# Chunked attention before two gated layers: its small products on all four 64x64 tiles of TensorE, on pairs of PSUM banks

## The chip, the cores and the metric

One core of a Trainium2 chip runs one program. The metric is the device time in microseconds (us); the profiled execution is a further run of the same program, of which the trace keeps every instruction. PE is TensorE's matrix multiply, PEld its weight load, DVE VectorE, ACT ScalarE, POOL GpSimd and SP SyncE, which issues the DMAs.

## The reference

The attention is a linear recurrence per head (4 batches, 8 heads, 768 steps, 48 numbers per head), and its output goes through two gated layers:

```python
for t in range(S):
    state = alpha[:, :, t, :, None] * state + np.einsum('bhd,bhe->bhde', k[:, :, t], v[:, :, t])
    y[:, :, t] = np.einsum('bhd,bhde->bhe', q[:, :, t], state)
x = y.transpose(0, 2, 1, 3).reshape(B * S, H * D)      # 3072 x 384
h = x @ w_in;  x = (h * np.cos(h)) @ w_out             # 384 -> 2048 -> 384
out = ((x @ w_a) * (x @ w_b)) @ w_o                    # 384 -> 1536 -> 384
```

The first line of the loop decays the state and adds the outer product of k and v of step t.

## The kernel before

**Units.** The recurrence is done in chunks of 64 steps. A unit is one chunk of one batch with all eight heads, as four pairs of heads (`NP`): 48 units, 12 chunks to a batch (`NCH`). One head of a pair lies on SBUF partitions 64 to 111, the other on 0 to 47 (`HEADS`). VectorE makes the running products of alpha with two scans (L289, L301), GpSimd scales q (L313), and k is scaled on VectorE in the first eight units and on GpSimd after (L326).

**Small products of a unit on TensorE** (K is the rows contracted, M the columns of weights loaded):
- T, the transposes of k (L359): 8 products, absent in a batch's last chunk, which leaves no state
- S, the scores of k with q (L369 and L372, a line per head of the pair): 8 products
- N, the new keys with v (L431, L432): 8 products, absent in a batch's last chunk
- Y, the outputs (L447, and L451 with the old state where it is carried on its own): 8 or 16 products
- O, the old state added by a product with the identity (L435): 1 product

These are float32, and each product stands in the trace as two matmuls. In T, S and N a product takes one 64x64 quarter of the array: the head on the upper partitions writes the lower half of PSUM's partitions or the other way round, so that of the four quarters two are used, on a diagonal. Y uses all rows of the array and half its columns.

**Banks.** T and N of a unit lie in one PSUM bank (`tu`), S and Y in another (`sy`); odd units of the first eight use two accumulator banks in their place (`tags`, L342). ACT reads T (copy of k, L364) and Y (L548, high part of x); DVE reads S (masking, L398 or L405), N (decay of the state L500, or an add L515) and Y (low part of x, L551).

**Kinds of units.** Units 0 to 15 (`APART`) carry the state apart (`s_t`); from unit 16 on the state stands in the rows of v that a unit's products read anyhow, so that there is no O and no L451. Units 0 to 7 are done first, since layer one needs 512 steps at once. From unit 8 on a unit is a *block* on TensorE, emitted in one go between the large products: Y of unit u, then T and S of unit u+1, then N and O of unit u (L473).

**Large products.** 3072 columns in six groups of 512 (`NG`). Layer one has 16 steps a group, each with nine 128x128x512 products into `hp` (L645) and nine into the accumulators (L652), with ACT and DVE making h cos(h) in between (L695 to L714). The first two steps of the first group are cut into halves of 256 columns, of which the first needs units 0 to 3 and the second units 4 to 7 (`mm_part`, L674). Weights arrive as 64-bit words and are converted by ACT, DVE and POOL (L588 to L625) while the first group runs. Layer two has 12 steps of 27 products.

**What sets the order.** Every operation is recorded with an estimated duration, its dependencies and a due time (`Plan`, L65), and a list scheduler writes out one fixed order per engine. At run time each engine works through its order and waits where something isn't ready. An operation whose estimate or dependencies are changed can so move others.

Of the kernel before, what the change touches and what calls it, by code (L numbers as in the profile page):

```python
# [51 lines left out]
IN_COLS = W_A + 2 * NE4  # L52
# [114 lines left out]
def chunked(ctx: ExitStack, tc: tile.TileContext, u_in: bass.AP, wts: bass.AP, out: bass.AP, in_range: bass.AP):  # L167
# [23 lines left out]
    mask = att.tile([P, 1, C], F32, name="mask", bufs=1)  # L191
    nc.gpsimd.memset(mask, 1.0)
    for r0 in (0, 64):
        nc.gpsimd.affine_select(
            out=mask[r0:r0 + 64], in_=mask[r0:r0 + 64], pattern=[[0, 1], [1, C]],
            compare_op=ALU.is_ge, fill=0.0, base=0, channel_multiplier=-1,
        )
# [63 lines left out]
    def plan_load(u):  # L261
# [3 lines left out]
        def load():  # L265
# [5 lines left out]
            cuts = (0, NA + 1, IN_COLS) if u == 0 else (0, IN_COLS)  # L271
# [70 lines left out]
    def tags(u):  # L342
        return ("acc1", "acc2") if u < UG and u % 2 else ("tu", "sy")

    def plan_scores(u, block=None):
        d, ops = un[u], U[u]
        apart = u < APART
        due = unit_due(u)
        m, kt = m_t[u % 3], k_t[u % 2]
        k, ma, m_before = ops["k"], ops["ma"], ops["m_before"]  # L350
        kp, kn_of = kt, kn_t[u % 2]
        state = u % NCH != NCH - 1
        tp = kn = None

        def transpose():
            d["tp"] = d["tu"][:, 0:NE4].rearrange("p (c e) -> p c e", e=D)
            for p in range(NP):
                for (rows, _), r0 in zip(HEADS, (0, 64)):
                    nc.tensor.matmul(  # L359
                        d["tp"][r0:r0 + 64, p, :], kp[rows, p, :], ident[rows, rows], start=True, stop=True  # L360
                    )

        def copy_k():
            nc.scalar.copy(kn_of[:, :, 0:D], d["tp"])  # L364

        def score():
            sc = d["sc"] = d["sy"][:, 0:256].rearrange("p (c t) -> p c t", t=C)
            for p in range(NP):
                nc.tensor.matmul(  # L369
                    sc[0:64, p, :], kp[64:112, p, :], m[64:112, 1 if apart else 0, p, :], start=True, stop=True  # L370
                )
                nc.tensor.matmul(  # L372
                    sc[64:128, p, :], kp[0:48, p, :], m[0:48, 2 if apart else 1, p, :], start=True, stop=True
                )

        def both():
            tu, sy = tags(u)
            d["tu"], d["sy"] = bank(tu, tu), bank(sy, sy)
            if state:
                transpose()  # L380
            score()

        if block is None:
            sc = op(PE, 0.95, both, [*k, *ma], due=due - 1.0)
            ops["tu"], ops["sy"] = (take(tag, 1, sc) for tag in tags(u))
        else:
            sc = block[0]
            need(sc, *k, *ma)
            ops["tu"], ops["sy"] = block[1:]
        ops["emit"] = ([transpose] if state else []) + [score]  # L390
        ops["k_last"] = [sc]
        if state:
            ops["kn"] = kn = op(ACT, 0.34, copy_k, [sc, *(U[u - 2]["us_op"] if u >= 2 else [])])
            ops["tu"] += [kn]
        if apart:
            mk = [op(
                DVE, 0.42,
                lambda: nc.vector.tensor_tensor(m[:, 0], d["sc"], mask.to_broadcast([P, NP, C]), op=ALU.mult),  # L398
                [sc, *m_before],
            )]  # L400
        else:
            mk = [
                op(
                    DVE, 0.42,
                    lambda r0=r0, i=i: nc.vector.tensor_tensor(  # L405
                        m[r0:r0 + 64, i], d["sc"][r0:r0 + 64], mask[r0:r0 + 64].to_broadcast([64, NP, C]), op=ALU.mult
# [706 lines left out]
```

## Time and profile before

| | us |
|---|---|
| median of 3 runs | 987.89 (987.19 to 987.96) |
| the profiled execution, own time | 988.87 |
| its span, first to last instruction | 987.2 |
| PE busy in it | 972.0 |
| DVE, ACT, POOL busy in it | 529.3, 407.6, 230.9 |

The span is 1.67 us less than the profiled execution's own time, and that execution is 0.98 us over the median. A busy share over the whole span says little here: the engines beside PE are busy in the first part and nearly idle in the last, so the profile is read by stretches.

### The profile page before, as it was taken

The numbers are of one execution on the slowest core, as the hardware profiler recorded it, in microseconds if no ns is written. First come the engines' busy times: TensorE is split into PE (matmuls) and PEld (weight loads), VectorE is DVE, ScalarE is ACT, GpSimd is POOL, SyncE is SP. The second block draws the span as 40 slices with busy tenths as digits, with TensorE's granted clock in tenths as the row PEclk, the third lists the DMA queues.
The fourth block names the chain that finished last, engine by engine and source line by source line (L and its number), as shares of the span: only waits on it lengthen the run. The fifth ranks groups of instructions, "written<-read, shape, count | busy, mean of one in ns | idle before, by whom it ended". The sixth has DMA issues, their size and how long they took to land.

```text
span 987.2 us, 16801 instructions
## 1 busy us (share of the span) xinstructions
PE 972.0 (98%) x6909; PEld 800.6 (81%) x6909; DVE 529.3 (54%) x887; ACT 407.6 (41%) x754; POOL 230.9 (23%) x259
## 2 busy tenths in 40 slices
PE   8899999999999999999999999999999999999996
PEld 6788888888888888888887888888888888888885
DVE  6998986766766676665877862222222222222221
ACT  4578854445445444544766532112112112112111
POOL 4556653313322322221323431001001001000000
PEclk8889999999999999999999999999999999999999
DMA  9355412112221211112223410000000000000000
GB/s 365 131 170 188 162 41 79 62 48 73 72 67 49 81 50 58 50 34 104 97 96 101 156 33 14 19 1 18 15 1 23 10 1 28 5 1 32 1 1 35
DMA packets 17700, 63.38 MB, mean 64 GB/s; under 512 B 2384, under 2 KB 4816, under 8 KB 17616
## 3 DMA queue, kind: packets, MB, share of 16 engines
q1 hardware_dynamic: 17616, 62.24, 18.3%
q8 instruction: 56, 0.92, 0.4%
q14 instruction: 28, 0.23, 0.1%
HBM read 55.15 MB, written 4.72 MB: 61 GB/s over the span
## 4 chain that ended last, share of the span: by engine, by line
PE 95%; DMA 2%; DVE 1%; SPq 0%; issue 0%; ACT 0%
PE acc L652 35%; PE hp L645 20%; PE bp L645 15%; PE ap L645 15%; PE sy L447 3%; PE tu L359 2%; PE sy L369 2%; DMA st_t<-wts 2%; PE tu L432 1%; DMA w_t<-u_in 1%; PE tu L431 1%; PE sy L451 0%; PE tu L435 0%; DVE wf_t L605 0%; DVE wf_t L599 0%; PE sy L372 0%
## 5 line engine op out<-in xcount | busy, mean ns | idle before, releaser
L652 PE MATMUL acc<-ghi_t,w_t 128*128 128x512 f32 x972 | 301.2, 391 | 0.0
L645 PE MATMUL hp<-x_t,w_t 128*128 128x512 f32 (+1 forms) x882 | 217.9, 392 | 3.1 <-DMA x_t<-x_t 3.1
L652 PEld LDWEIGHTS acc<-ghi_t,w_t 128*128 128x128 f32 x972 | 181.7, 188 | 37.7
L645 PEld LDWEIGHTS hp<-x_t,w_t 128*128 128x128 f32 x882 | 163.3, 191 | 37.0 <-issue 3.5
L808 DVE TENSOR_TENSOR bp<-c_t,bp 128x512 f32<-128x512 f32 x72 | 50.1, 695 | 262.0 <-PE bp L645 244.0
L652 PE MATMUL acc<-glo_t,w_t 128*128 128x512 f32 x486 | 189.3, 390 | 0.0
L645 PE MATMUL bp<-x_t,w_t 128*128 128x512 f32 x594 | 145.6, 389 | 0.0
L645 PE MATMUL ap<-x_t,w_t 128*128 128x512 f32 x540 | 132.2, 389 | 0.0
L645 PEld LDWEIGHTS bp<-x_t,w_t 128*128 128x128 f32 x594 | 111.5, 188 | 23.5
L645 PEld LDWEIGHTS ap<-x_t,w_t 128*128 128x128 f32 x540 | 101.4, 188 | 21.2
L805 ACT COPY c_t<-ap 128x512 f32<-128x512 f32 x72 | 42.3, 587 | 179.8 <-PE ap L645 179.6
L652 PEld LDWEIGHTS acc<-glo_t,w_t 128*128 128x128 f32 x486 | 91.2, 188 | 19.5
L812 ACT CAST ghi_t<-bp 128x512 fp32r<-128x512 f32 x72 | 42.3, 587 | 137.9 <-DVE bp L808 137.9
L768 POOL TENSOR_TENSOR x_t<-x,x_t 128x512 fp32r<-128x512 f32 x18 | 25.1, 1416 | 256.9 <-ACT x_t L765 256.9
L625 POOL TENSOR_TENSOR w_t<-wf_t,w_t 128x768 fp32r<-128x768 f32 x32 | 64.1, 2005 | 88.4 <-ACT w_t L614 78.7
L710 ACT CAST ghi_t<-hp 128x512 fp32r<-128x512 f32 x96 | 56.4, 587 | 68.2 <-DVE hp L706 67.3
L695 ACT ACTIVATE c_t<-hp 128x512 int32<-128x512 f32 x96 | 57.6, 600 | 58.1 <-PE hp L645 57.2
L698 DVE CUSTOM_DVE_ANT_0 c_t<-c_t,hp 128x512 f32<-128x512 int32 x96 | 65.6, 683 | 25.3 <-ACT c_t L695 24.9
L703 ACT ACTIVATE c_t<-c_t 128x512 f32<-128x512 f32 x96 | 60.4, 629 | 44.7 <-DVE c_t L698 44.2
L706 DVE TENSOR_TENSOR hp<-c_t,hp 128x512 f32<-128x512 f32 x96 | 65.9, 686 | 23.7 <-ACT c_t L703 23.2
L326 POOL TENSOR_TENSOR k<-ar_t,in_t 112x256 f32<-112x256 f32 x40 | 30.8, 769 | 201.8 <-PE sy L372 157.8
L714 DVE TENSOR_TENSOR glo_t<-hp,ghi_t 128x512 fp32r<-128x512 f32 x96 | 65.4, 681 | 18.4 <-ACT ghi_t L710 18.2
(110 smaller groups left out, 1094.2 us busy)
## 6 DMA issues: line engine op xcount, KB each, us to landing
st_t<-wts SPq DMA_DIRECT2D x34, 768.0 KB, 4.4
in_t<-u_in SPq DMA_DIRECT2D x40, 578.0 KB, 3.7
out<-o_t SPq DMA_DIRECT2D x18, 256.0 KB, 2.1
w_t<-u_in SPq DMA_DIRECT2D x7, 578.0 KB, 8.2
x_t<-x_t SPq DMA_DIRECT2D x48, 48.0 KB, 2.5
w_t<-u_in SPq DMA_DIRECT2D x1, 447.5 KB, 4.2
w_t<-u_in SPq DMA_DIRECT2D x1, 130.5 KB, 2.2
```

The costliest lines, as they stand in the source:

```text
L625: nc.gpsimd.tensor_tensor(t[:, 1], conv.pop(i), t[:, 0].bitcast(F32), op=ALU.subtract)
L645: nc.tensor.matmul(acc, wt[:, w, j * P:(j + 1) * P], r[:, j, :], start=i == 0, stop=i == len(terms) - 1)
L652: nc.tensor.matmul(accs[j], wt[:, w, j * P:(j + 1) * P], r, start=first and i == 0, stop=last and i == 2)
L695: nc.scalar.activation(s["c"].bitcast(I32), s["u"], AF.Identity, bias=-0.25, scale=-1.0)
L698: nc.vector._custom_dve(TENSOR_ADD_SAT, out=s["c"], in0=s["c"].bitcast(I32), in1=s["u"], s0=0.25, s1=-0.75)
L703: nc.scalar.activation(s["c"], s["c"], AF.Sin, bias=math.pi / 2, scale=TWO_PI)
L706: nc.vector.tensor_tensor(s["u"], s["c"], s["u"], op=ALU.mult)
L710: nc.scalar.copy(s["hi"], s["u"])
L714: nc.vector.tensor_tensor(s["lo"], s["u"], s["hi"].bitcast(F32), op=ALU.subtract)
L805: nc.scalar.copy(s["c"], s["a"])
L808: nc.vector.tensor_tensor(s["b"], s["c"], s["b"], op=ALU.mult)
L812: nc.scalar.copy(s["hi"], s["b"])
```

## The change

T, S and N are spread over all four quarters of the array. The four pairs of heads become two halves `b` of two pairs `c`; in half 1 a head's products write the other half of PSUM's partitions (`rows_of`), and each half has a PSUM bank of its own, which holds S, T, N and Y of that half. The first eight units take two such sets of two banks in turn (`xy`, and two of the accumulators), later ones `xy`. The order of products runs over the quarters. v of two pairs is then needed on other rows: units from 16 on load 96 more columns (`again`). O is cut in two products of 96 columns instead of one of 192, since it now lies in two banks. The masking from unit 16 on is four DVE operations of 64x128 instead of two of 64x256. Of the first eight units N, O and Y are one operation of the plan. S now stands ahead of T. Since ACT and DVE now read the same two banks, their reads are put in one fixed order: copy of k (of the next unit, in a block), high part of x, then masking and decay or add, with the low part after the high part. Names follow: `tu`, `sy` and the accumulator tags become `xy` and `acc_t`. Estimates of the plan change with it.

```diff
-IN_COLS = W_A + 2 * NE4
+IN_COLS = W_A + 2 * NE4 + 2 * D
...
+    xy = ps.tile([P, 2, G], F32, name="xy", bufs=1)
+    acc_t = ps.tile([P, KT, G], F32, name="acc_t", bufs=1)
+    banks = [
+        [
+            t[:, :, c0:c0 + 2 * n].rearrange("p b (c t) -> p b c t", c=2)
+            for c0, n in ((0, C), (2 * C, D), (2 * C + 2 * D, D), (2 * C + 4 * D, C))
+        ]
+        for t in (xy, acc_t[:, 1:3])
+    ]
+
+    def banks_of(u):
+        return banks[u % 2 if u < UG else 0]
...
+    def rows_of(b, h):
+        return slice(0, 64) if (b + h) % 2 == 0 else slice(64, 128)
...
+        def score():
+            for c in range(2):
+                for b in range(2):
+                    for rows, h in HEADS:
+                        nc.tensor.matmul(
+                            sc_t[rows_of(b, h), b, c, :], kt[rows, 2 * b + c, :],
+                            m[rows, h + apart, 2 * b + c, :], start=True, stop=True,
+                        )
...
-        ops["emit"] = ([transpose] if state else []) + [score]
+        ops["emit"] = [score] + ([transpose] if state else [])
...
+        first = [ops.get("kn"), U[u - 1]["ys_read"][0] if block is not None else None]
...
+            def masked(b, h):
+                rows, to = rows_of(b, h), rows_of(0, h)
+                nc.vector.tensor_tensor(
+                    m[to, h, 2 * b:2 * b + 2], sc_t[rows, b], mask[rows, 0].to_broadcast([64, 2, C]), op=ALU.mult
                 )
+            ops["mk"] = [
+                op(DVE, 0.24, lambda b=b, h=h: masked(b, h), [sc, *m_before, *first])
+                for b in range(2) for h in range(2)
             ]
...
+            for c in range(2):
+                for b in range(2):
+                    first = not carry or c == 0
+                    for rows, h in HEADS:
+                        r, p = rows_of(b, h), 2 * b + c
+                        v = again[r, c] if b and not apart else vs(u, h)[r, p]
+                        n = C if apart and h else D
+                        nc.tensor.matmul(
+                            us_t[rows.start:rows.start + n, b, c, :], kn_of[r, p, 0:n], v, start=first, stop=not carry
+                        )
+
+        def old_state():
+            for b in range(2):
+                nc.tensor.matmul(
+                    us_t[0:112, b].rearrange("p c e -> p (c e)"), ident, s_t[u % 2][:, b * 2 * D:(b + 1) * 2 * D],
+                    start=False, stop=True,
+                )
...
+            us = ou = op(PE, 1.75 if carry else 0.85, part, [kn, ld, *mk, *ma, *before], due=due)
...
-            us = ou = op(PE, 2.35 + (0.8 if carry else 0.0), block, [kn, ld, *mk, *ma, *before], due=due)
+            us = ou = op(PE, 1.75 + (1.0 if carry else 0.0), block, [kn, ld, *mk, *ma, *before], due=due)
...
+            need(xh, U[u + 1].get("kn"))
+
+
+        first = [xh, U[u + 1].get("kn") if u >= UG and u + 1 < NU else None]
...
+                    op(DVE, 0.36, lambda n=n: decay(carried(u + 1)[n]), [us, ld_next, *before, *first], due=due + 1.0)
```

What stands in a block of a unit from 16 on, on PE, before: Y, T x8, S with a line per head, N with a line per head, between large products (`hp`, L645).

```order
L447 MATMUL sy<-m_99,in_t 48x64
L359 MATMUL tu<-ident,k_107 64x48 x8
L369 MATMUL sy<-m_100,k_107 64x64
L372 MATMUL sy<-m_100,k_107 64x64
...
L431 MATMUL tu<-in_t,kn_110 48x48
L432 MATMUL tu<-in_t,kn_110 64x48
...
L645 MATMUL hp<-x_t,w_t 128x512 x9
```

The same place on PE after (L461 is Y, L374 S, L383 T, L444 N, L656 the large product):

```order
L461 MATMUL xy<-m_101,in_t 64x64
L461 MATMUL xy<-m_101,in_t 48x64
L374 MATMUL xy<-m_99,k_107 64x64 x8
L383 MATMUL xy<-ident,k_107 64x48 x8
L444 MATMUL xy<-in_t,kn_110 48x48 x8
L656 MATMUL hp<-x_t,w_t 128x512 x9
```

The counts are the same; S and T have changed places, and all eight of N now load 48 columns of weights, where four loaded 64.

PE at the end of the first eight units, before: the end of unit 6, unit 7 whole (`acc_551`), then both halves of the first step's `hp` (18 matmuls of 256 columns), then unit 8.

```order
L451 MATMUL sy<-m_99,s_105 48x64
L660 LDWEIGHTS zeros
L660 MATMUL acc_121<-zeros 64x512
L435 MATMUL acc_550<-s_106,ident 112x192
L447 MATMUL acc_551<-m_100,w_t 64x64
...
L645 MATMUL hp<-x_t,w_t 128x256 x18
L359 MATMUL tu<-ident,k_107 64x48 x8
```

The same place on PE after (unit 7 is the one with `k_108` and `m_100`):

```order
L466 MATMUL xy<-m_99,s_105 48x64
L671 LDWEIGHTS zeros
L671 MATMUL acc_t<-zeros 64x512
L374 MATMUL acc_t<-m_100,k_108 64x64 x8
L383 MATMUL acc_t<-ident,k_108 64x48 x8
L656 MATMUL hp<-x_t,w_t 128x256 x9
L444 MATMUL acc_t<-w_t,kn_110 48x48
L444 MATMUL acc_t<-w_t,kn_110 64x48
...
L450 MATMUL acc_t<-s_106,ident 112x96 x2
L461 MATMUL acc_t<-m_100,w_t 64x64
```

The first half of the first `hp` now stands between the scores and the rest of unit 7; the second half comes after the scores of unit 8.

DVE in the first step of layer one, before (L698 and L706 are the step's first two operations on DVE, L714 its third, L301 a scan):

```order
L698 ISA c_t<-c_t,hp 128x512
L289 SCALAR_TENSOR_TENSOR ar_t<-in_t,first 112x260
L298 RECIPROCAL last<-ar_t 112x4
L398 TENSOR_TENSOR m_101<-sy,mask 128x256
L301 SCALAR_TENSOR_TENSOR ar_t<-in_t,last 112x260
L706 TENSOR_TENSOR hp<-c_t,hp 128x512
```

The same place on DVE after (L709, L717 and L725 for L698, L706 and L714; L315 the scan):

```order
L616 SCALAR_TENSOR_TENSOR wf_t<-st_t,wf_t 128x768
L312 RECIPROCAL last<-ar_t 112x4
L709 ISA c_t<-c_t,hp 128x512
L717 TENSOR_TENSOR hp<-c_t,hp 128x512
L315 SCALAR_TENSOR_TENSOR ar_t<-in_t,last 112x260
L725 TENSOR_TENSOR glo_t<-hp,ghi_t 128x512
```

The scan that stood ahead of the step's second operation now stands behind it, and ahead of the third.

## Rows read from the trace of the kernel before

**Rows 1.** Busy time by stretches (us, count), TensorE's clock, DMA share, GB/s:
```profile
core 0: us, PE busy (x) PEld busy (x) DVE busy (x) ACT busy (x) POOL busy (x), PEclk, DMA share, GB/s
0.00:53.00 53.00, 45.55 (x794) 36.33 (x794) 43.07 (x81) 24.56 (x53) 29.31 (x40) 0.83 0.62 233
53.00:130.00 77.00, 77.00 (x779) 64.70 (x778) 70.52 (x111) 60.41 (x108) 47.43 (x33) 0.98 0.51 170
130.00:455.00 325.00, 325.00 (x3037) 267.35 (x3036) 222.06 (x431) 156.55 (x323) 94.19 (x151) 1.00 0.18 57
455.00:530.00 75.00, 75.00 (x332) 62.11 (x331) 56.56 (x83) 48.61 (x79) 20.63 (x11) 1.00 0.33 119
530.00:987.00 457.00, 449.49 (x1975) 370.14 (x1973) 137.11 (x184) 117.45 (x196) 39.36 (x25) 1.00 0.07 23
```

**Rows 2.** The page's chain that ended last, by line, shares of the span:
```profile
PE acc L652 35%; PE hp L645 20%; PE bp L645 15%; PE ap L645 15%; PE sy L447 3%; PE tu L359 2%; PE sy L369 2%; DMA st_t<-wts 2%; PE tu L432 1%; DMA w_t<-u_in 1%; PE tu L431 1%; PE sy L451 0%; PE tu L435 0%; DVE wf_t L605 0%; DVE wf_t L599 0%; PE sy L372 0%
```

**Rows 3.** Timeline of PE, one block: start, duration, line, tile, K*M, shape, count:
```profile
227.60 0.68 PE L447 MATMUL sy<-m,in_t 112*64 112x64 f32 x16
228.21 0.67 PE L359 MATMUL tu<-ident,k 48*64 48x48 f32 x16
228.71 0.23 PE L369 MATMUL sy<-m,k 48*64 48x64 f32 x1
228.71 0.23 PE L372 MATMUL sy<-m,k 48*64 48x64 f32 x1
228.78 0.22 PE L369 MATMUL sy<-m,k 48*64 48x64 f32 x1
...
229.13 0.22 PE L369 MATMUL sy<-m,k 48*64 48x64 f32 x1
...
229.19 0.20 PE L432 MATMUL tu<-in_t,kn 64*64 64x48 f32 x1
229.19 0.20 PE L431 MATMUL tu<-in_t,kn 64*48 64x48 f32 x1
...
229.51 0.20 PE L431 MATMUL tu<-in_t,kn 64*48 64x48 f32 x1
229.52 0.28 PE L432 MATMUL tu<-in_t,kn 64*64 64x48 f32 x2
229.73 0.50 PE L645 MATMUL hp<-x_t,w_t 128*128 128x512 f32 x1
```

**Rows 4.** Timeline of PE, the end of a block with O:
```profile
109.56 0.58 PE L435 MATMUL tu<-s,ident 112*112 112x192 f32 x2
109.85 0.77 PE L652 MATMUL acc<-ghi_t,w_t 128*128 128x512 f32 x2
```

**Rows 5.** Groups of instructions on DVE by shape: busy us, mean ns:
```profile
L405 DVE TENSOR_TENSOR m<-sy,mask 64x256 f32<-64x256 f32 x64 | 26.7, 418 | 1.6 <-PE sy L372 0.6 <-ACT x_t L548 0.5
L515 DVE TENSOR_TENSOR sm_t<-tu,in_t 48x192 f32<-48x192 f32 x58 | 20.6, 355 | 25.4 <-PE tu L432 21.3 <-ACT kn L364 3.1
```

**Rows 6.** Timeline of the first eight units, the state's chain:
```profile
20.27 0.33 DVE L500 TENSOR_TENSOR s<-tu,ar_t 112x192 f32<-112x192 f32 x1
...
29.82 0.58 PE L435 MATMUL acc<-s,ident 112*112 112x192 f32 x2
30.33 0.33 PE L447 MATMUL acc<-m,w_t 112*64 112x64 f32 x4
31.55 0.39 ACT L548 ACTIVATE x_t<-acc 112x256 fp32r<-112x256 f32 x1 [2.00 <-PE acc L451]
...
37.41 0.35 DVE L500 TENSOR_TENSOR s<-acc,ar_t 112x192 f32<-112x192 f32 x1
```

**Rows 7.** Timeline around the first step of layer one, waits in brackets:
```profile
36.09 1.84 POOL L625 TENSOR_TENSOR w_t<-wf_t,w_t 128x768 fp32r<-128x768 f32 x1 [4.42 <-ACT w_t L614]
38.48 1.34 PE L645 MATMUL hp<-x_t,w_t 128*128 128x256 f32 x9
42.88 2.26 PE L645 MATMUL hp<-x_t,w_t 128*128 128x256 f32 x9 [3.05 <-DMA x_t<-x_t]
47.62 4.17 DVE L301 TENSOR_TENSOR_SCAN ar_t<-in_t,last 112x260 f32<-112x260 f32 x1
51.71 0.67 DVE L706 TENSOR_TENSOR hp<-c_t,hp 128x512 f32<-128x512 f32 x1
```

More of the change, by code (lines that the diff above doesn't have):

```diff
@@ L363, in copy_k @@
-        def copy_k():
[L364 to L374, printed above, removed]
@@ L383, in plan_scores @@
+        before = []
+        if block is None and u >= 2:
+            before = [*U[u - 2]["read"]] if u < UG else [*U[u - 2]["read"], *U[u - 1]["read"]]
         if block is None:
-            sc = op(PE, 0.95, both, [*k, *ma], due=due - 1.0)
-            ops["tu"], ops["sy"] = (take(tag, 1, sc) for tag in tags(u))
-        else:
-            sc = block[0]
-            need(sc, *k, *ma)
-            ops["tu"], ops["sy"] = block[1:]
-        ops["emit"] = ([transpose] if state else []) + [score]
+            sc = op(PE, 0.6, lambda: [fn() for fn in ops["emit"]], [*k, *ma, *before], due=unit_due(u) - 1.0)
+        else:
+            sc = block
+            need(sc, *k, *ma, *before)
@@ L447, in outputs @@
                     nc.tensor.matmul(
-                        y, w[0:k_rows, cols], m[0:k_rows, 0 if apart else i, p, :], start=True, stop=not carry
+                        ys_t[r0:r0 + n, b, c, :], w[0:k_rows], m[0:k_rows, 0 if apart else h, p, :],
+                        start=True, stop=not carry,
                     )
@@ L560, in plan_back, with last_a, decay, add @@
         need(xh, E["xfirst", g] if off else None)
+        ops["ys_read"] = [xh]
+        if u >= UG and u + 1 < NU:
+            plan_scores(u + 1, us)
+            need(xh, U[u + 1].get("kn"))
+        first = [xh, U[u + 1].get("kn") if u >= UG and u + 1 < NU else None]
+        ops["us_read"] = []
+        if state:
+            ld_next = plan_load(u + 1) if u + 1 >= APART else None
+            def last_a(rows):
+                return by_bank(d["a"])[rows, :, :, C:SEP].to_broadcast([rows.stop - rows.start, 2, 2, D])
+            if apart:
+                def decay(new):
+                    rows, new = new
+                    nc.vector.tensor_tensor(by_bank(new), us_t[rows], last_a(rows), op=ALU.mult)
+                before = [*U[u - 1]["ou"], U[u - 1]["us"]] if u else []
+                dc = ops["us_read"] = [
+                    op(DVE, 0.36, lambda n=n: decay(carried(u + 1)[n]), [us, ld_next, *before, *first], due=due + 1.0)
+                    for n in range(2 if u + 1 >= APART else 1)
+                ]
+            else:
+                def add(rows, i):
+                    if "sm" not in d:
+                        d["sm"] = att.tile([112, NP, D], F32, name="sm_t")
+                    nc.vector.tensor_tensor(by_bank(d["sm"][rows]), us_t[rows], by_bank(vs(u, i)[rows]), op=ALU.add)
+                def decay(rows, i):
+                    nc.gpsimd.tensor_tensor(
+                        vs(u + 1, i)[rows], d["sm"][rows], d["a"][rows, :, C:SEP].to_broadcast([48, NP, D]), op=ALU.mult
+                    )
+                ad = ops["us_read"] = [
+                    op(DVE, 0.36, lambda r=r, i=i: add(r, i), [us, ld, *U[u - 1].get("dc", []), *first])
+                    for r, i in HEADS
+                ]
+                need(ad[1], ad[0])
+                sm_last = take("sm", 2, ad[0])
+                dc = [
+                    op(POOL, 0.52, lambda r=r, i=i: decay(r, i), [ad[n], ld_next], port=True, due=due + 1.0)
+                    for n, (r, i) in enumerate(HEADS)
+                ]
+                sm_last += dc
+                in_last += ad
+            ops["dc"] = dc
+            ar_last += dc
@@ L903, in chunked @@
         )
-        count = op(PE, 0.1, count_good, [E["late"]])
-        take("tu", 1, count)
+        E["count"] = op(PE, 0.1, count_good, [E["late"]])
         for g in range(NG):
```

198 lines of the change are left out of this document (67 added, 131 removed).

## The prediction

> **What bounds the kernel now.** I read the stretches first, then the chain that ended last, then one block of a unit instruction by instruction. By the stretches [rows 1] the execution has four parts. Up to 53 us nothing is full for long. From 53 to 530 us PE is busy all the time, and after it 449.5 of 457 us. So from 53 us on the end is set by what PE has to do, and the chain says the same: its large shares are PE lines, and the small products of the attention (L359, L369, L372, L431, L432, L435, L447, L451) have about 10% of it [rows 2]. The reader should look at DVE beside PE: 92% busy from 53 to 130 us (70.5 of 77.0), 68% from 130 to 455 us (222.1 of 325). In the second stretch a shorter PE block shortens the end; in the first, DVE stands close behind.
>
> In one block without O [rows 3] Y takes 0.61 us (227.60 to 228.21), T 0.50, S 0.48, N 0.54 (to 229.73), in all 2.13 us. The pace inside is what matters. In S the two quarters start within 0.01 us of each other, and each then starts a matmul every 58 ns (L369 from its second, 228.78, to its eighth, 229.13: six steps in 0.35 us). T streams 48 columns where S streams 64, and takes the same time; both load 64 columns of weights. In N one quarter loads 48 and the other 64, with equal streams: L431 runs eight matmuls with 46 ns steps (229.19 to 229.51), L432 has only its seventh at 229.52. So a quarter has a pace of its own, set by the weights it loads, and does not wait for its neighbour. That is the basis of the forecast.
>
> **The change part by part.**
>
> *S, T and N on four quarters.* Each quarter gets four matmuls instead of eight. S and T: 8 x 58 = 466 ns becomes 4 x 58 = 233 ns, a gain of 0.233 us each. N from unit 16 on loads 48 columns throughout: 466 ns (the 64-column quarter ends last) becomes 4 x 46 = 183 ns, a gain of 0.283 us. In units below 16 one head keeps 64 columns, a gain of 0.233 us. Two quarters that share rows, or that share columns, do not appear together in S, T and N before; Y runs two tiles on the same rows at once (16 matmuls in 0.61 us, eight per tile at 58 ns being 0.47), so that weights and streams from shared rows are covered by a row. Two tiles on the same columns are covered by none. Bounds: a gain of nothing, to the full halves. I take the halves, since the tiles of rows 3 run independently in all else, less what two more starts cost: with starts up to 0.01 us apart, 0.013 us a phase (0 to 0.03).
>
> The rows show no four quarters at once. The Trainium skill, "TensorE: Matmul & The Clock Gate", Part 3 (packing small matmuls), says that row and column tiles compose and that each further tile adds about 4 ns; no run here shows it yet, and by it the starts would cost 0.7 us in the sum below in place of 1.2.
>
> Counts from 130 to 455 us: the blocks of units 16 to 47 hold 31 S (units 17 to 47), 28 T (without units 23, 35, 47) and 29 N: 31 x 0.233 + 28 x 0.233 + 29 x 0.283 = 22.0 us, less 88 x 0.013 = 1.2, so **20.8 us**. PE is full there and DVE is not, so I count all of it.
>
> *Units 9 to 15, from 53 to 130 us.* 7 S, 6 T and 6 N at 0.233 make 4.4 us. O in two products: four weight loads of 112 columns instead of two, half the stream each. The next large product starts 0.29 us after O does [rows 4], so two more loads cost between 0 and about 0.2 us; I take 0.1, five times, 0.5 us. Left are 3.9 us of PE. In a stretch 3.9 us shorter DVE would be 96% busy, in a fixed order with waits on ACT; I count half, **2.0 us**. Against it works the new order of readers: mask and decay now wait for ACT's copy of k and high part of x. The high part takes 0.39 us [rows 6] and the copy has fewer columns, so at most 0.78 us a unit stands on DVE with the next steps' operations queued behind, 7 x 0.78 = 5.5 us if all of it showed. Range here: 3.9 gained to 5.5 lost.
>
> *The same waits after 130 us* meet DVE at 68%, with some 10 us between two blocks (32 in 325 us): nothing. Masking becomes four operations: from 418 ns for 256 columns and 355 for 192 [rows 5], 128 columns are about 0.29 us (an estimate from these two); 4 x 0.29 - 2 x 0.418 = 0.33 us a unit, 10.6 us in all, which makes DVE 77% busy in the shorter stretch. Hidden by DVE's idle time; if that were gone, it would cost up to 10.6 us. Loads grow by 96 columns on 1156, 8%, on a DMA share of 0.18 [rows 1]: nothing. In 455 to 987 us nothing changes, and the conversion of layer two's weights, which waits for the attention's end, moves forward with it.
>
> *Up to 53 us.* Two edits pull. First, the decay of a unit now waits for the high part, so from O's start the state's chain is 31.55 - 29.82 + 0.39 + 0.35 and about 0.1 for hand-overs, 2.6 us a unit [rows 6]. Decays came every 3.43 us (20.27 to 37.41, five units), so this does not bind by itself. Second, the first half of the first `hp` is moved ahead of unit 7's N, O and Y. It needs POOL's part of the first weights, done at 36.09 + 1.84 = 37.93 us [rows 7]; then unit 7 ends at about 37.93 + 1.34 + 2.0 (1.73 from O to the high part, and N) = 41.3 us instead of before 38.48, and the second half, which waited for unit 7's rows by DMA at 42.88, comes near 45.6. What is late next is DVE: there the step's second operation stood behind a scan of 4.17 us until 51.71. Now the scan stands behind it: 45.6 + 2.26 + three operations of ACT and DVE at 0.6 to 0.7 with hand-overs make about 50.5, and the scan then delays the third operation, by 0.7 to 4.2 us. The two cancel within what I can see: 0, with 3 us either way.
>
> **Sum.** Span 987.2 - 20.8 - 2.0 - 0 = 964.4 us. The median of the runs is 0.69 us over the profiled span (987.89 against 987.2; the profiled execution itself took 988.87). So **965.0 us** (965.1, rounded), with 960 to 971 for this case alone.
>
> **The rivals.**
>
> *DVE takes the first 130 us.* If the waits on ACT show in full and the start loses its 3 us, the first two stretches lose 8.5 us rather than gain 2.0: 987.9 - 20.8 + 8.5 = 975.6 us. For it speaks DVE at 92%; against it, that the planner has put ACT's reads first and DVE has other work to place between.
>
> *A floor on starts.* If the queue cannot start matmuls faster on four quarters than it is ever seen to on two, the fastest mean is N's, 16 in about 0.39 us, 24 ns each [rows 3]. Then S, T and N cost 0.39 us instead of 0.466: (88 + 19 / 2) x 0.075 = 7.3 us, 980.6 us. For it: no row is faster on average. Against: single starts stand 0.01 us apart, and N's 24 ns are just what quarters at 46 and 58 ns give. The Trainium skill, same page, section "Wait — 56ns, not 53.3ns?", says that start-to-start never drops below about 25 ns; the trace's starts 0.01 us apart disagree for single ones and leave the mean open. By 25 ns a phase is 0.40 us and the time 981.5 us.
>
> *No gain from shared columns.* If two tiles that write the same columns take turns, S, T and N keep their 0.466 us: 988 us, no change.
>
> *Slower: turns with a price.* The order of products changes quarters in pairs, three times inside a phase. A change of tile shape costs 0.14 us at Y's end (0.61 against 8 x 58) and 0.07 at N's (0.54 against 0.466) [rows 3]. If shared columns exclude each other and each turn costs 0.07 us, a phase grows by 0.21: 107 x 0.21 = 22 us, 1010 us. With full overlap it would decide from 0.233 / 3 = 0.078 us a turn. Against it: all three phases have one shape.
>
> **How the numbers follow.** Forecast 0.70; DVE in the first 130 us 0.11; floor 0.09; no gain 0.04; turns 0.06. The predicted time is the forecast's. From 960 to 976 us the range holds nearly all of the first and most of the second, about 0.8. A measurement of this kernel can tell about 0.2% (2 us) from no change: faster 0.90 (the first three), same 0.04, slower 0.06.
>
> **What would show it.** In a block from unit 16 on: S and T near 0.25 us, N near 0.2 plus the step to the large product, the block near 1.4 us instead of 2.13, and four starts in each 58 ns; 24 ns a start would show the floor, 58 ns for each pair the turns. PE full from 130 us on, and that stretch near 304 us. From 53 to 130 us: DVE's share, and PE waits behind the glo part of a step. At the start: the second half of the first `hp` near 45 us, and the steady stream of large products from 53 us, 3 either way. The prediction is wrong if the quarters slow each other, or if PE shows waits for masks or states after 130 us.

## The result and the profile after

The changed kernel takes 973.58 us (median of 4 runs, 973.26 to 974.9) against 987.77 us for the kernel before in the same group of runs: a ratio of 0.986, 95% interval 0.9843 to 0.9877. So it is 14.2 us faster, where 22.9 were forecast. The time lies inside the range given, but 8.6 us above the predicted one, next to the 975.6 us of the rival "DVE takes the first 130 us".

The stretches after, with the columns of [rows 1]:

```profile
0.00:53.00 53.00, 39.05 (x828) 30.65 (x829) 40.77 (x82) 24.47 (x55) 26.77 (x40) 0.90 0.62 234
53.00:130.00 77.00, 70.25 (x762) 55.82 (x761) 73.35 (x105) 56.44 (x101) 46.85 (x34) 1.00 0.49 170
130.00:455.00 325.00, 323.88 (x3124) 262.23 (x3123) 245.25 (x518) 166.38 (x342) 96.95 (x153) 1.00 0.21 69
455.00:530.00 75.00, 74.76 (x330) 61.31 (x329) 57.83 (x82) 48.28 (x78) 24.80 (x13) 1.00 0.31 106
530.00:971.00 441.00, 431.94 (x1899) 356.28 (x1897) 123.31 (x168) 107.62 (x180) 31.11 (x21) 0.99 0.06 20
```

From 130 us on PE is all but full, as before: 1.1 us are missing there, up to 142 us, and behind that it waits 0.2 us in all. From 53 to 130 us it no longer is full: 70.25 of 77.0, where before it had all 77.0, while DVE went from 92% to 95%. The page's chain by line says the same: DVE's lines on the weights (L610, L616) and on the step (L709) now have 1% each, where [rows 2] has the weights' at 0%.

```profile
PE acc_t L663 33%; PE hp L656 18%; PE xy L656 15%; PE ap L656 15%; PE xy L461 2%; DMA st_t<-wts 2%; PE xy L374 1%; DVE wf_t L610 1%; DVE wf_t L616 1%; DMA w_t<-u_in 1%; PE xy L383 1%; DVE c_t L709 1%; DVE ar_t L303 1%; PE xy L444 1%; DVE gl
```

One block of a unit from 16 on, PE's timeline (the block of [rows 3] after the change; L461 is Y, L374 S, L383 T, L444 N), then what the trace has on line L383 in this window:

```profile
147.15 0.68 PE L461 MATMUL xy<-m,in_t 112*64 112x64 f32 x16
147.76 0.46 PE L374 MATMUL xy<-m,k 48*64 48x64 f32 x16
148.04 0.40 PE L383 MATMUL xy<-ident,k 48*64 48x48 f32 x16
148.26 0.36 PE L444 MATMUL xy<-in_t,kn 64*48 64x48 f32 x16
148.55 0.50 PE L656 MATMUL hp<-x_t,w_t 128*128 128x512 f32 x1
```

```profile
L383 PE MATMUL xy<-ident,k x16: 204/218/219, 148.0 to 148.2; 48*64 48x48 f32 x16
```

Read the differences of the starts: Y 0.61 us, S 0.28, T 0.22, N 0.29, in all 1.40 us against 2.13. Sixteen matmuls of T go off in 0.22 us, 14 ns each in the mean.

The whole difference can be laid out on three points of the program. The first block from unit 16 on begins at 141.43 us, before at 137.73: 3.7 us **later**. Its Y on PE, after and then before:

```profile
141.43 0.68 PE L461 MATMUL xy<-m,in_t 112*64 112x64 f32 x16
```

```profile
137.73 0.68 PE L447 MATMUL sy<-m,in_t 112*64 112x64 f32 x16
```

From there to the Y of the last block it takes 294.80 us, before 316.29: 21.5 us less. From that Y to the last product both kernels take 525.7 us. From the last product to the end it takes 9.46 us (961.94 to 971.4), before 7.47 (979.73 to 987.2): 2.0 us more. 3.7 - 21.5 + 2.0 = -15.8, which is the difference of the spans (971.4 - 987.2). It is 1.6 us more than the 14.2 of the medians, since the profiled execution of the kernel before lies above its median and the one after slightly below.

The 3.7 us hide two terms. The first large product into the accumulators starts *earlier* than before, at 52.99 us instead of 56.29 (after, then before):

```profile
52.99 0.63 PE L663 MATMUL acc_t<-ghi_t,w_t 128*128 128x512 f32 x2
```

```profile
56.29 0.63 PE L652 MATMUL acc<-ghi_t,w_t 128*128 128x512 f32 x2
```

From there to unit 16's block it then takes 88.4 us instead of 81.4: the stretch in which layer one runs beside units 9 to 15 has grown by 7.0 us. Of the 3.3 us gained ahead of it, about 1 is the clock's. In the kernel before, PE was busy 1.8 of the 4 us up to 42 us, and from 42 to 53 us its granted clock was 0.50, the lower of its two levels (1.2 and 2.4 GHz), from 53 to 56 us 0.61 in the mean. The 18 products of the second step took 3.35 us there (52.94 to 56.29). After, at a granted clock of 0.98 (50 to 53 us), they take 2.23 us (50.76 to 52.99).

So three questions stand: is the gain from 141 us on the quarters' alone, what takes the time ahead of 141 us, and what takes it at the end.

**The first 141 us.** Four groups of DVE's instructions by shape tell where its time is (count, busy us, mean ns, idle before). After, from 53 to 142 us:

```profile
L610 DVE SCALAR_TENSOR_TENSOR wf_t<-wf_t,st_t 128x768 int32<-128x768 int32 x13 | 18.9, 1454 | 0.1
L616 DVE SCALAR_TENSOR_TENSOR wf_t<-st_t,wf_t 128x768 int32<-128x768 int32 x13 | 15.4, 1184 | 0.0
L303 DVE TENSOR_TENSOR_SCAN ar_t<-in_t,first 112x260 f32<-112x260 f32 x9 | 9.4, 1045 | 0.0
L315 DVE TENSOR_TENSOR_SCAN ar_t<-in_t,last 112x260 f32<-112x260 f32 x9 | 7.1, 792 | 0.0
```

The same four lines before, from 53 to 138 us:

```profile
L605 DVE SCALAR_TENSOR_TENSOR wf_t<-st_t,wf_t 128x768 int32<-128x768 int32 x13 | 15.9, 1221 | 0.2
L599 DVE SCALAR_TENSOR_TENSOR wf_t<-wf_t,st_t 128x768 int32<-128x768 int32 x13 | 13.2, 1012 | 0.1
L301 DVE TENSOR_TENSOR_SCAN ar_t<-in_t,last 112x260 f32<-112x260 f32 x9 | 7.0, 783 | 0.1
L289 DVE TENSOR_TENSOR_SCAN ar_t<-in_t,first 112x260 f32<-112x260 f32 x9 | 6.8, 755 | 0.0
```

The instructions and their counts are the same, and the change touches none of them, yet they take 50.8 us instead of 42.9. Left alone, the weights' operations take about 0.945 us (0.92 at the least, 0.95 in the median) and the scans 0.69, which would be 26 x 0.945 + 18 x 0.69 = 37.0 us. What lies above that, 13.8 us after and 5.9 before, is called the *excess* below. A place where it arises, DVE and then POOL after the change:

```profile
77.01 2.98 DVE L610 SCALAR_TENSOR_TENSOR wf_t<-wf_t,st_t 128x768 int32<-128x768 int32 x1
```

```profile
76.68 0.69 POOL L340 TENSOR_TENSOR k<-ar_t,in_t 112x256 f32<-112x256 f32 x1 [1.87 <-DVE ar_t L315]
77.32 1.86 POOL L636 TENSOR_TENSOR w_t<-wf_t,w_t 128x768 fp32r<-128x768 f32 x1
```

DVE's L610 is issued while POOL works, and it ends at 79.99, 0.81 us after POOL's second operation (77.32 + 1.86 = 79.18). It stands still for about 2 us; the profile counts that as busy time of DVE, not as a wait. DVE operations with one input in PSUM (L709, L717, L725, means of 0.67 to 0.68 us) never show it: none takes over 0.70 us. The Trainium skill, "SBUF — State Buffer", section "SBUF: two separate sides", says that a DVE operation with two inputs in SBUF and a GpSimd operation that reads SBUF exclude each other: the one that starts first has the shared ports for its whole instruction, and the other waits. The rows agree (2.98 us where 0.945 is usual); here, moreover, DVE stands still over two POOL instructions in a row.

PE's waits by line from 53 to 142 us (us in total, times, longest), where before there is none:

```profile
PE acc_t L663 <- DVE glo_t L725: 3.8, 5, 1.7
PE xy L461 <- issue: 1.8, 1, 1.8
PE xy L374 <- POOL m L327: 1.2, 2, 1.0
PE acc_t L663 <- ACT ghi_t L721: 1.0, 2, 0.8
```

**The end.** Engines' timeline after, the last product and the three drains of the accumulators:

```profile
961.56 0.39 PE L663 MATMUL acc_t<-glo_t,w_t 128*128 128x512 f32 x1
961.98 0.60 ACT L864 ACTIVATE o_t<-acc_t 128x512 f32<-128x512 f32 x1 [2.73 <-PE acc_t L663]
962.61 0.69 DVE L862 TENSOR_SCALAR o_t<-acc_t 128x512 f32<-128x512 f32 x1 [2.63 <-ACT o_t L864]
963.34 0.60 ACT L864 ACTIVATE o_t<-acc_t 128x512 f32<-128x512 f32 x1 [0.76 <-DVE o_t L862]
```

and before:

```profile
978.40 0.60 ACT L850 ACTIVATE o_t<-acc 128x512 f32<-128x512 f32 x1 [1.36 <-PE acc L652]
979.08 0.69 DVE L848 TENSOR_SCALAR o_t<-acc 128x512 f32<-128x512 f32 x1 [1.32 <-PE acc L652]
979.34 0.39 PE L652 MATMUL acc<-glo_t,w_t 128*128 128x512 f32 x1
979.76 0.60 ACT L850 ACTIVATE o_t<-acc 128x512 f32<-128x512 f32 x1 [0.77 <-PE acc L652]
```

Before, each accumulator is drained as soon as its own nine products are done. After, all three are one tile (`acc_t`), so that the first drain waits for the last product of all, and each further one for the drain ahead of it: the last begins 1.40 us after PE's end instead of 0.03.

### The profile page after: what moved, and what is told of

The parts are those of the page before. It is cut to its first block, busy times and chain, and to the rows that moved or that the text cites. A ratio compares the mean times of both kernels' runs of the same rounds, so it can differ in the third digit from the quotient of the medians.

```text
span 971.4 us, 16849 instructions
## 1 busy us (share of the span) xinstructions
PE 939.9 (97%) x6935; PEld 766.3 (79%) x6935; DVE 540.5 (56%) x951; ACT 403.2 (42%) x754; POOL 226.5 (23%) x259
## 4 chain that ended last, share of the span: by engine, by line
PE 87%; DVE 6%; DMA 2%; ACT 2%; issue 1%; POOL 1%; SPq 0%; ACTq 0%
PE acc_t L663 33%; PE hp L656 18%; PE xy L656 15%; PE ap L656 15%; PE xy L461 2%; DMA st_t<-wts 2%; PE xy L374 1%; DVE wf_t L610 1%; DVE wf_t L616 1%; DMA w_t<-u_in 1%; PE xy L383 1%; DVE c_t L709 1%; DVE ar_t L303 1%; PE xy L444 1%; DVE glo_t L725 1%
## 5 line engine op out<-in xcount | busy, mean ns | idle before, releaser
L663 PE MATMUL acc_t<-ghi_t,w_t 128*128 128x512 f32 x972 | 301.1, 391 | 1.0 <-ACT ghi_t L721 1.0
L656 PE MATMUL hp<-x_t,w_t 128*128 128x512 f32 (+1 forms) x882 | 216.4, 390 | 3.2 <-DMA x_t<-x_t 3.2
L663 PEld LDWEIGHTS acc_t<-ghi_t,w_t 128*128 128x128 f32 x972 | 181.6, 188 | 39.3 <-ACT ghi_t L721 1.9
L663 PE MATMUL acc_t<-glo_t,w_t 128*128 128x512 f32 x486 | 190.1, 391 | 3.8 <-DVE glo_t L725 3.8
L822 DVE TENSOR_TENSOR xy<-c_t,xy 128x512 f32<-128x512 f32 x72 | 50.1, 696 | 258.0 <-PE xy L656 257.9
L656 PEld LDWEIGHTS hp<-x_t,w_t 128*128 128x128 f32 x882 | 161.1, 188 | 36.8 <-ACT w_t L625 3.3
L656 PE MATMUL xy<-x_t,w_t 128*128 128x512 f32 x594 | 145.6, 390 | 0.0
L656 PE MATMUL ap<-x_t,w_t 128*128 128x512 f32 x540 | 132.2, 389 | 0.0
L656 PEld LDWEIGHTS xy<-x_t,w_t 128*128 128x128 f32 x594 | 111.5, 188 | 23.4
L656 PEld LDWEIGHTS ap<-x_t,w_t 128*128 128x128 f32 x540 | 101.4, 188 | 21.1
L663 PEld LDWEIGHTS acc_t<-glo_t,w_t 128*128 128x128 f32 x486 | 91.2, 188 | 25.6 <-DVE glo_t L725 6.4
L826 ACT CAST ghi_t<-xy 128x512 fp32r<-128x512 f32 x72 | 42.2, 586 | 138.3 <-DVE xy L822 138.3
L706 ACT ACTIVATE c_t<-hp 128x512 int32<-128x512 f32 x96 | 57.5, 599 | 67.4 <-PE hp L656 67.1
L714 ACT ACTIVATE c_t<-c_t 128x512 f32<-128x512 f32 x96 | 60.6, 631 | 46.7 <-DVE c_t L709 45.9
L709 DVE CUSTOM_DVE_ANT_0 c_t<-c_t,hp 128x512 f32<-128x512 int32 x96 | 65.6, 683 | 25.6 <-ACT c_t L706 24.7
L717 DVE TENSOR_TENSOR hp<-c_t,hp 128x512 f32<-128x512 f32 x96 | 65.8, 685 | 19.7 <-ACT c_t L714 19.2
L830 DVE TENSOR_TENSOR glo_t<-xy,ghi_t 128x512 fp32r<-128x512 f32 x72 | 49.8, 692 | 47.3 <-ACT ghi_t L826 47.3
L725 DVE TENSOR_TENSOR glo_t<-hp,ghi_t 128x512 fp32r<-128x512 f32 x96 | 65.7, 684 | 17.1 <-ACT ghi_t L721 16.3
```

Of the source, the lines that this page charges most:

```text
L656: nc.tensor.matmul(acc, wt[:, w, j * P:(j + 1) * P], r[:, j, :], start=i == 0, stop=i == len(terms) - 1)
L663: nc.tensor.matmul(accs[j], wt[:, w, j * P:(j + 1) * P], r, start=first and i == 0, stop=last and i == 2)
L706: nc.scalar.activation(s["c"].bitcast(I32), s["u"], AF.Identity, bias=-0.25, scale=-1.0)
L709: nc.vector._custom_dve(TENSOR_ADD_SAT, out=s["c"], in0=s["c"].bitcast(I32), in1=s["u"], s0=0.25, s1=-0.75)
L714: nc.scalar.activation(s["c"], s["c"], AF.Sin, bias=math.pi / 2, scale=TWO_PI)
L717: nc.vector.tensor_tensor(s["u"], s["c"], s["u"], op=ALU.mult)
```

## The experiments

The theory after this first reading, **frozen by POOL**: from 53 to 141 us DVE is the bound, and it loses 8 us more than before by standing still beside POOL's reads, so that the shorter blocks of units 9 to 15 bring nothing. Its main rival, **waits on ACT**, is the prediction's own second case: masking and decay stand behind ACT's copy and high part in the new fixed order of readers.

### The quarters alone undone

```
-        return slice(0, 64) if (b + h) % 2 == 0 else slice(64, 128)
+        return slice(0, 64) if h == 0 else slice(64, 128)
...
-                        v = again[r, c] if b and not apart else vs(u, h)[r, p]
+                        v = vs(u, h)[r, p]
```

The order of every engine stays word for word that of the changed kernel. In units 0 to 15 half 1's keys and scores then meet v of the pair's other head; the work is the same.

> The changed kernel with only the quarters undone: the second half of the pairs writes the same rows of PSUM as the first, so that S, T and N run on two quarters of the array again; banks, loads, plan and the order on every engine stay as in the changed kernel. If the quarters' gain is real and fully on the path from 130 us on, a block from unit 16 on goes from 1.40 back to about 2.1 us and the time rises by about 22 us, with little more from the units before (DVE, not PE, sets the pace there): 995 to 997 us. If PE's length counted in the first 130 us too, 4 us more: 1000. If only part of the shorter block reaches the end, under 990. What this kernel has over the kernel before (987.8) is then the price of all the rest of the change: about 8 us.

Measured: 998.25 us, ratio to before 1.0103 (1.0086 to 1.012). A block, PE's timeline:

```profile
157.83 0.68 PE L461 MATMUL xy<-m,in_t 112*64 112x64 f32 x16
158.43 0.68 PE L374 MATMUL xy<-m,k 48*64 48x64 f32 x16
158.95 0.62 PE L383 MATMUL xy<-ident,k 48*64 48x48 f32 x16
159.40 0.53 PE L444 MATMUL xy<-in_t,kn 64*48 64x48 f32 x16
159.86 0.50 PE L656 MATMUL hp<-x_t,w_t 128*128 128x512 f32 x1
```

S 0.52, T 0.45, N 0.46: the block is 2.03 us. From unit 16's block to the last product it takes 839.1 us, in the changed kernel 820.5, before 842.0. So of the 21.5 us gained there 18.6 come from the quarters, and 2.9 are there without them, most of it N's, at 48 columns of weights throughout: 0.46 us instead of 0.54. The rest of the expectation missed: unit 16's block begins at 151.45 us, 10.0 later than with four quarters, where at most 4 were expected. A longer PE does count in the first stretch, also ahead of 53 us (the first large product starts at 42.77 instead of 37.63). Without the quarters, the rest of the change makes the kernel about 10 us slower than before. That loss is in the first stretch, where this run's excess is 16.5 us (the changed kernel's is 13.8, and 15.8 when it is run again). What else is lost there isn't taken apart by any run.

### POOL's part of the weights without its reads

```
-            nc.gpsimd.tensor_tensor(t[:, 1], conv.pop(i), t[:, 0].bitcast(F32), op=ALU.subtract)
+            w = conv.pop(i)
+            if i < NPAIR1:
+                nc.gpsimd.memset(t[:, 1].bitcast(F32), 0.0)
+            else:
+                nc.gpsimd.tensor_tensor(t[:, 1], w, t[:, 0].bitcast(F32), op=ALU.subtract)
```

> The changed kernel, but POOL's part of the first 16 pairs of weights (the low part, a product of two SBUF inputs) only writes zeros, so the low parts of layer one's weights are left out of the result. Theory 'frozen by POOL': in the changed kernel DVE operations with two SBUF inputs stand still while POOL does this operation (eight of them took 2.0 to 3.3 us instead of 0.7 to 0.95), on a DVE that is 95% busy. Then these long ones go, DVE's excess from 50 us on falls from 14.7 us to 6 or less, unit 16's block begins 4 to 7 us earlier than 141.4, and the time is about 968 us (966 to 970). Rival 'waits on ACT' (the fixed order of readers holds DVE and PE up): unit 16's block stays within 1 us of 141.4 and the time within 1.5 us of 973.6.

The same edit in the kernel before:

> The same edit in the kernel before (low parts of layer one's weights left out). There the excess of DVE's operations was 6.6 us from 50 us on and PE was busy all the time from 53 us on. 'Frozen by POOL': little to gain since PE sets the end there, 0 to 2 us: 986 to 988; the difference between the kernels then grows from 14.2 to 18 or more. 'Waits on ACT': no change here, and the difference between the kernels stays 14.

and in the changed kernel with the memset three times over:

> As lo_quiet, but POOL writes the zeros three times over, which takes it about 2.2 us a pair of weights (three of 0.735) where the real operation took 1.99: POOL is as busy as in the changed kernel and its part of the weights is as late, but it reads no SBUF there (low parts of layer one's weights left out again). 'Frozen by POOL's reads': as lo_quiet, 966 us (964 to 968), excess of DVE's operations from 50 us on about 2.4 us. Rival 'POOL's time or the later weights': back near 973.6.

Measured: 966.01 us (ratio to before 0.9788, 0.9769 to 0.9808) for the first, 988.73 (0.9995, 0.9983 to 1.0007) in the kernel before, 967.24 (0.9782, 0.9753 to 0.9811) for the threefold one. DVE's groups in `lo_quiet_long`, from 53 to 142 us, and POOL's memsets, up to 142 us:

```profile
L610 DVE SCALAR_TENSOR_TENSOR wf_t<-wf_t,st_t 128x768 int32<-128x768 int32 x13 | 13.5, 1036 | 0.1
L616 DVE SCALAR_TENSOR_TENSOR wf_t<-st_t,wf_t 128x768 int32<-128x768 int32 x13 | 12.8, 987 | 0.0
...
L315 DVE TENSOR_TENSOR_SCAN ar_t<-in_t,last 112x260 f32<-112x260 f32 x9 | 6.7, 750 | 0.0
L303 DVE TENSOR_TENSOR_SCAN ar_t<-in_t,first 112x260 f32<-112x260 f32 x9 | 6.2, 689 | 0.0
```

```profile
L639 POOL MEMSET w_t<- 128x768 f32 x48 | 35.2, 739 | 1.8
```

The excess is 39.2 - 37.0 = 2.2 us instead of 13.8, with POOL as long at work (35.2 us for 16 pairs; the real operation takes 31.8). Unit 16's block begins at 135.84 us (132.74 in `lo_quiet`, more than was expected) instead of 141.43, and PE is 76.0 of 77.0 us busy from 53 to 130 us. From the first product into the accumulators to unit 16's block it takes 80.1 us in `lo_quiet` and 80.2 in `lo_quiet_long`, against 88.4 in the changed kernel, 88.8 when that is run again, and 81.4 in the kernel before. So it is the reads of the weights that cost, not POOL's time. In the kernel before the same edit takes the excess from 5.9 to about 2 us and moves nothing, 81.4 us again: there PE set the end, and DVE's standing still was covered.

With these reads gone, the changed kernel gains 22 us on the kernel before. That this is so near the 22.9 forecast is partly luck: in the execution of `lo_quiet` unit 16's block comes 5.0 us earlier than before, where 2.0 was forecast, and the end takes 1.7 us more, where nothing was.

### The order of readers taken out of the plan

```
-        first = [ops.get("kn"), U[u - 1]["ys_read"][0] if block is not None else None]
+        first = []
...
-        first = [xh, U[u + 1].get("kn") if u >= UG and u + 1 < NU else None]
+        first = []
```

> The changed kernel without the fixed order of readers in the plan: masking, decay and add no longer stand behind ACT's copy of k and high part of x there. The order on every engine changes with it, to that of a plan without these waits. Rival 'waits on ACT' (5.5 us of waits in the first 130 us): unit 16's block 4 to 6 us earlier and about 968 us. 'Frozen by POOL': the waits on ACT are not the cost; within 3 us of the changed kernel either way, by how often DVE and POOL meet in the new order.

Measured: 987.98 us (the median of nine runs, 982 to 996; a tenth, at 997, is left aside; ratio 0.9987, 0.9947 to 1.0026), beside 975.35 us for the changed kernel again in the same group:

> The changed kernel itself, as the ground of this group of runs: 973.6 us as before, within 2 us, with several of DVE's operations on two SBUF inputs at 2 to 3.3 us between 45 and 125 us.

Both theories missed by far. Without the order the scores of the next unit no longer stand ahead of a unit's N, O and Y among the first eight, the units run one after the other, and the first large product starts at 50.53 us instead of 37.63. The total can't price the waits; it shows that the plan's knowledge of the readers is worth some 13 us in the first units. A part of that may be the clock's, granted at 0.74 up to 53 us here and at 0.81 in the changed kernel run again. But the stretch behind the start can be compared: from the first product into the accumulators (68.44 us) to unit 16's block it takes 87.9 us, against 88.4 and 88.8 with the order. The waits' rival would have it 4 to 6 us shorter. The changed kernel's own trace agrees: from 53 to 140 us DVE waits 3.3 us in all, less than the 6.6 before, and only 1.6 of it is the decay behind ACT's high part:

```profile
DVE s L535 <- ACT x_t L505: 1.6, 2, 0.9
DVE c_t L709 <- ACT c_t L706: 1.5, 2, 0.9
DVE glo_t L725 <- ACT ghi_t L721: 0.2, 1, 0.2
```

### The accumulators in three tiles again

```
+    accp = ExitStack()
-    acc_t = ps.tile([P, KT, G], F32, name="acc_t", bufs=1)
+    acc_t = accp.enter_context(tc.tile_pool(name="accp", bufs=1, space=PSUM)).tile(...)
...
-                acc[g] = [acc_t[:, j] for j in range(KT)]
+                if g == 0:
+                    accp.close()
+                    accs.append(ctx.enter_context(tc.tile_pool(name="accs", bufs=1, space=PSUM)))
+                acc[g] = [accs[0].tile([P, G], F32, name=f"acc{j}", bufs=1) for j in range(KT)]
```

> The changed kernel with the three accumulators as three tiles again from the first step of layer one on (the first eight units keep the joint tile). If the joint tile is why the last three drains start after the last product of all three and then one after another, the first drain starts about 1.4 us before the last product's end again, the stretch from the last product to the end shrinks from 9.4 to about 7.5 us, and the time is 971.6 us (971.2 to 972.0). If the drains are held by something else: 973.6.

Measured: 974.17 us, ratio 0.9855 (0.9838 to 0.9873). The drains, ACT and DVE at the end:

```profile
963.89 0.60 ACT L868 ACTIVATE o_t<-acc 128x512 f32<-128x512 f32 x1 [1.36 <-PE acc L664]
964.59 0.69 DVE L866 TENSOR_SCALAR o_t<-acc 128x512 f32<-128x512 f32 x1 [1.33 <-PE acc L664]
964.84 0.39 PE L664 MATMUL acc<-glo_t,w_t 128*128 128x512 f32 x1
965.26 0.60 ACT L868 ACTIVATE o_t<-acc 128x512 f32<-128x512 f32 x1 [0.77 <-PE acc L664]
```

The last drain is back at 0.03 us behind PE's end (965.23), so 1.37 us of the tail were the joint tile's. The stretch from PE's end to the end of the span is 8.3 us, not 7.5: the stores behind the last drain took 7.6 us here, 6.8 before and 7.5 in the changed kernel. So 0.6 of the 2.0 us are the stores', which vary from run to run: they took 6.8 when the changed kernel was run again. The total can't show 1.4 us: in this execution unit 16's block began at 144.56 us, 3.1 later than in the changed kernel's, and 143.51 in the changed kernel run again. The first stretch scatters by that much.

### Versions that let DVE in

Four pieces in place of POOL's one operation, with the three tiles:

```
+            w, n = conv.pop(i), 2 * DM // 4
+            for c in range(0, 2 * DM, n):
+                nc.gpsimd.tensor_tensor(
+                    t[:, 1, c:c + n], w[:, c:c + n], t[:, 0, c:c + n].bitcast(F32), op=ALU.subtract
+                )
```

> A version meant to keep what the change gains: POOL's part of the weights in four pieces of 192 columns, so that a DVE operation that meets it waits for one piece (about 0.6 us) and not for 1.85 to 2.0, and the accumulators in three tiles from the first step of layer one on. 'Frozen by POOL': DVE's excess from 50 us on falls from 14 us to 6 to 9, unit 16's block begins 3 to 6 us earlier than in the changed kernel, and the drains give 1.4 us: 967 us (965 to 970). If short pieces only make DVE wait more often: excess as before and 972.2, the drains alone.

Measured: 971.73 us, ratio 0.9826 (0.9802 to 0.9849), with 975.35 us and 0.9868 (0.9847 to 0.9889) for the changed kernel beside it. It is 3.6 us below the changed kernel beside it and leaves nothing out; 1.4 of the 3.6 are the drains'. The pieces did less than expected, excess 11.8 us beside the 15.8 of the changed kernel in this group. DVE and POOL at one place:

```profile
77.98 3.65 DVE L611 SCALAR_TENSOR_TENSOR wf_t<-wf_t,st_t 128x768 int32<-128x768 int32 x1
```

```profile
77.92 0.68 POOL L341 TENSOR_TENSOR k<-ar_t,in_t 112x256 f32<-112x256 f32 x1
78.57 2.25 POOL L639 TENSOR_TENSOR w_t<-wf_t,w_t 128x192 fp32r<-128x192 f32 x4
```

Here DVE is not let in between POOL operations that follow each other: it stands still from 77.98 through all five. Two runs put a short write of POOL's ahead of each piece, `nc.gpsimd.memset(gap, 0.0)`, the second with six pieces and a shorter write:

> As pieces_tail, but ahead of each of the four pieces POOL writes 64 columns of a tile that nobody reads, so that pieces of 0.56 us are parted by some 0.15 us in which POOL reads no SBUF. In pieces_tail a DVE operation that met POOL's work stood still to the end of all of POOL's operations that followed each other without a break (3.4 and 3.65 us). 'Frozen by POOL's reads, let in at a break': the long ones go, none over about 2 us, excess from 50 us on 5 to 8 us instead of 11.8, unit 16's block 3 us or more earlier than in pieces_tail, 968 us (966 to 970). If a waiting DVE operation isn't let in at such a break: as pieces_tail, 971.7, or later by POOL's 0.6 us a pair of weights.

> As gaps_tail with six pieces of 128 columns and shorter breaks (16 columns written): pieces of about 0.43 us, so a met piece costs DVE less, but the break is about 0.1 us. If any break lets DVE in: excess 4 to 7 us and 967 us (965 to 969). If a break has to be as long as in gaps_tail: excess near 11.8 and 971 to 973.

Measured: 974.83 us (0.9863, 0.9842 to 0.9883) and 975.04 (0.9852, 0.9828 to 0.9876). Both missed, with an excess of 10 and 9 us. At 52.31 us of `gaps_tail` DVE got in at a break; its operation issued at 76.53 took 4.0 us, standing still through four breaks of 0.14 us. When a break lets DVE in stays open.

The last run held POOL to its place in the plan. There operations of the two that exclude each other never meet (the port flag of an operation); in the trace DVE is 1 to 3 us behind the plan and POOL 0 to 2.

```
+            if "out" in o.get("behind", {}):
+                nc.gpsimd.tensor_copy(seen, o["behind"]["out"]().bitcast(I32))
             o["fn"]()
```

> The changed kernel with the accumulators in three tiles (as tail_three) and with POOL held to its place in the plan: up to 135 us, a POOL operation that reads SBUF waits for the DVE operation on two SBUF inputs that the plan puts last ahead of it, by a copy of one column of what that wrote. In the plan such operations of the two engines never meet; in the trace DVE runs 1 to 3 us behind the plan and POOL's part of the weights 0 to 2, so that POOL comes first and DVE stands still. 'Frozen by POOL': most meetings go, DVE's excess from 50 us on falls from 14 us to 4 to 7, unit 16's block begins at 134 to 138 us instead of 141.4 or later, and the time is 966 us (964 to 969), about as in lo_quiet, with every product in place. If DVE stands still because POOL's work has to be done beside it in any order: excess 10 or more and 971 to 975.

Measured: 971.52 us, ratio 0.9834 (0.9807 to 0.986), which can't be told from the four pieces' 0.9826. The excess stayed at 13 us; there are more meetings, and shorter ones: from 53 to 142 us 13 operations of 1.2 us or more, the longest 2.6, where the changed kernel has 8, up to 3.0. So the drift between the engines is not the whole reason why they meet. In the trace POOL's work, once held, often falls on DVE's next operation of the kind. Undisturbed, DVE's operations of this kind and POOL's reads need some 75 us of the 88 from 53 us to unit 16's block (an estimate: DVE 25 x 0.86 + 18 x 0.61, from one start to the next; POOL 14 x 1.85 + 24 x 0.68). That leaves little room in any order; that no order avoids the meetings isn't shown. A way around it that keeps every product wasn't found.

## Why the prediction was right, and where it was not

**S, T and N on four quarters: right.** Forecast 20.8 us from 130 us to the end of the attention, measured 21.5, of which the runs give 18.6 to the quarters and 2.9 to the rest of the change, most of it N's columns. By the forecast's own terms these were 19.3 and 1.5, so a little of the match is luck. S 0.28, T 0.22 and the block at 1.40 us are what was named. Two tiles on the same columns of the array, for which there was no row before, don't disturb each other here: each keeps its pace of 58 ns.

**The floor on starts, no gain, turns with a price: all three fell.** A phase is 0.22 to 0.29 us, not 0.39, 0.466 or more. The Trainium skill, "TensorE: Matmul & The Clock Gate", section "Wait — 56ns, not 53.3ns?", has 25 ns as the least from start to start; with small products on four tiles this trace shows 14 ns in the mean.

**Units 9 to 15 and the start: this is the step that failed.** The prediction took 2.0 us off there and 0 for the start; unit 16's block came 3.7 us later, 5.7 us from the forecast. PE's own work did shrink nearly as the term said: in `lo_quiet_long`, where little holds it up, the seven blocks of units 9 to 15 take 14.7 us, before 18.3, 3.6 less against a forecast of 3.9. The start went better than forecast: the second half of the first `hp` came at 45.72 us (45.6 was worked out), and the first products into the accumulators at 52.99 instead of 56.29. But from 53 us to unit 16's block PE then stood idle for 7.9 us, and "steady from 53 us, 3 either way" was wrong: PE still has gaps up to unit 16. So the term of 2.0 us gained in this stretch was 7.0 us lost, and the start's 3.3 us hid a part of it.

The step that failed is "DVE 92% busy", taken as work. It was 92% with 5.9 us of standing still, which cost nothing as long as PE was the bound. The sign was in [rows 7]: a scan of 4.17 us, where the same scan takes 0.69 alone. It was used as a duration, and its cause not asked for. POOL's L625, which [rows 7] shows at an earlier place only, ran twice beside that scan (47.62 to 51.24):

```profile
47.62 3.62 POOL L625 TENSOR_TENSOR w_t<-wf_t,w_t 128x768 fp32r<-128x768 f32 x2
```

**The rival that came closest had the place right and the mechanism wrong.** DVE did take the first 130 us, at 975.6 us forecast against 973.6, but by POOL, not by waits on ACT: those were 1.6 us for the decay where up to 5.5 were allowed, and the start lost nothing. That its number came so close is luck: it had 8.5 us lost up to unit 16's block, where 3.7 were, and nothing at the end, where 2.0 were. Without POOL's reads of the weights the same kernel, with the same waits on ACT, is at 966 to 967 us, 1 to 2 us from the forecast of 965.0.

**"In 455 to 987 us nothing changes": wrong by 2.0 us,** 1.37 of them shown to be the joint accumulator tile. The diff had it (`acc_t`), and it was read as a change of names.

**The smaller terms held.** Masking takes 0.286 us an operation (0.29 was estimated from [rows 5]) and is hidden from 141 us on, where PE waits 0.2 us in all, for another operation. O in two products costs 0.13 us more each, not 0.1.

## What to carry to other kernels

Before counting on a second engine's idle time, look at the spread of its durations: an instruction with a mean of 1.45 us and single ones of 3 us, where it takes 0.945 alone, meant here that the engine stood still inside its busy time, and the shorter bound on PE turned that into a later end. The PSUM tile joined from several banks for one user's sake also joined the waits of the others, down to the last drain. Small products are worth spreading over all four quarters of the array: here the 8 products of S went from 0.48 to 0.28 us and those of T from 0.50 to 0.22, though the tiles shared rows and columns.

## What had not been expected of the hardware

- A DVE operation with two SBUF inputs that meets POOL's reads wasn't let in between POOL operations that follow each other: 3.65 us through five of them, and 4.0 us through four breaks of 0.14 us with a write alone.
- Four tiles start 7 ns apart (T's first four at 148.045, .052, .059 and .064 us), so that starts cost 0.02 us a phase where 0.013 was taken. Each tile then keeps its own pace: the next four of T at 148.090, then every 58 ns; N's fours, with 48 columns of weights, every 43 to 47 ns.
